# A squared relu moved from PSUM to SBUF, two copies moved to another engine, and the order of interleaved jobs changed, in an RWKV-7 and feed-forward kernel

## The chip, the cores and the metric

The kernel runs on one core of one Trainium2 chip. The metric is the device time of one execution in microseconds (us). A result is the median of several executions, with the lowest and highest beside it. Times are compared only between kernels that ran in turn on the same chip in the same rounds. All executions reported here were of the fast state.

Five engines work side by side: PE (TensorE, with PEld for its weight loads), DVE (VectorE), ACT (ScalarE), POOL (GpSimd) and SP, which here only issues transfers.

## The reference

There are two stages. A recurrence runs over 768 steps for 4 batches and 8 heads with head size 40. Then a feed-forward layer works on the 3072 tokens that come out of it.

```python
for t in range(S):
    y[:, :, t] = einsum('bhd,bhde->bhe', rt, state)
    Sa = einsum('bhde,bhe->bhd', state, at)
    state = state * wt[:, :, None, :] - einsum('bhd,bhe->bhde', Sa, bt)
    state = state + einsum('bhd,bhe->bhde', vt, kt)
x = y.transpose(0, 2, 1, 3).reshape(3072, 320)
h = maximum(x @ w_in, 0)          # w_in: 320 x 2048
out = (h * h) @ w_out             # w_out: 2048 x 320
```

## The kernel before

The sequence is cut into chunks of 128 steps, so there are 24 pairs of chunk and batch. The main loop takes them one after the other in 24 *slots*. A slot runs several generators, called jobs here, in twelve steps. In each step the jobs take their turns in the order of the list, so the list sets the order of instructions in every engine's queue.

```python
    for i in range(len(order)):
        n, begin = share.get(i, (10, 0))
        g = ready.pop(i)
        jobs = [(chain(i, g), 11, 0, TOTAL) if i else (first_slot, 10, 0, TOTAL)]
        if i + 1 < len(order):
            if i:
                ready[i + 1] = {}
                load(i + 1, ready[i + 1])
            jobs.append((rest(i + 1, ready[i + 1]), 9, 2, TOTAL))
        made = ahead.get(i, ())
        for j, m_ in enumerate(made):
            jobs.append((prepare(m_), 5, j * 5, TOTAL - 5 * (len(made) - 1 - j)))
        done.update(made)
        jobs.append((some(second, n), n, begin, TOTAL))
        # ... (one more piece in the first slots)
        weave(*jobs)
```

- `chain(i)` is the serial part of this chunk: products with a precomputed inverse T, two pairs of copies to `minus_x`/`xr`, the masked product RX, the outputs y. For y it needs RX and this chunk's own RV, which `rest` made one slot earlier.
- `rest(i + 1)` makes what the next chunk needs: kvT, the masked products A and RV, the state's update.
- `prepare(m)` makes the decay factors of a later chunk. What it makes goes to POOL, which solves for the inverses T of several chunks at a time and writes them out (`kept_t`).
- `some(second, n)` is a piece of the feed-forward layer. Slots 0 to 3 have none.

The feed-forward piece and the copies, before:

```python
                ps = [psum(ps_f ...)[:, :GB * C] for _ in range(2)]        # two PSUM banks
                for e, p_ in enumerate(ps):
                    mm(p_, w_third[half, ...], t_[half, NT, :], True)       # half-height: two at a time
                for e, p_ in enumerate(ps):
                    for j in range(NT):
                        mm(p_, w_in[:, j, ...], t_[:, j, :], False)
                    h_ = hidden[:, f + e]
                    nc.scalar.activation(h_, p_, Act.Relu)                  # L663
                    nc.vector.tensor_tensor(h_, p_, h_, Alu.mult)           # L664: reads the bank again
# in chain:
            nc.scalar.copy(xn[halves[half], ::2, :D], xs[halves[half]])             # L592
            nc.vector.tensor_copy(xn[halves[half], 1::2, :D], xs[halves[1 - half]]) # L593
# in rest:
        nc.vector.tensor_tensor(kT, kT_, down[:, :, 1:C + 1], Alu.mult)     # L503: kvT
```

In the profile's lines `L87` is the helper `mm`, `L311` the transposing helper, and `L327` the helper that masks A, RV and RX.

## Time and profile before

| | before |
|---|---|
| median of 3 runs (range) | 1071.65 us (1070.01 to 1072.65) |
| profiled span, mean granted clock | 1071.7 us, 0.904 |
| PE held up at w_third by the product L664 | some 30 groups, 21.5 us |
| PE held up by RX's masks | 22 waits of weight loads, 22.3 us |
| stretches at half clock between 310 and 960 us | 8 |

The page cuts the span into 40 slices of 26.8 us and gives the busy tenths of each. PEclk is the granted TensorE clock in tenths of full speed. Three rows of the kernel before:

```profile
PE   6267656769999999999999999999999999999898
POOL 4788555885886899932999921999958860000000
PEclk8657655688999999899899999999999999999899
```

PE is full from the tenth slice on, so from there PE's order and stalls set the time. POOL works in bursts up to the thirty-third slice; it is no bound as long as its inverses come in time. The isolated 8 in PEclk are slices in which the clock was halved for a while. PE does not become idle there, but slower. The prediction below shows the other lines.

### The profile page before, as it was taken

To read this page: it belongs to the slowest core of one execution; us is meant where nothing else is said; L and a number is where in the kernel's file an instruction comes from. 1 tells how busy PE (TensorE), PEld (TensorE's weight loads), DVE (VectorE), ACT (ScalarE), POOL (GpSimd) and SP (SyncE) were. 2 spreads that over 40 slices of the span, in tenths; PEclk is the share of its full clock that TensorE was granted. 3 is DMA by queue.
4 is the path that set the end of the run, shared out by engine and by line. 5 is a ranking of instruction groups with operands and counts; after the bars stand their busy time and mean duration, and the time that the engine had idled before them with its cause. 6 is when DMAs were issued, how large, how long until landed. Compare 5 with 4: busy or idle time off the path is not lost.

```text
span 1071.7 us, 19693 instructions
## 1 busy us (share of the span) xinstructions
PE 952.1 (89%) x7824; PEld 678.6 (63%) x7824; DVE 498.6 (47%) x1012; ACT 251.9 (24%) x555; POOL 650.2 (61%) x1124
## 2 busy tenths in 40 slices
PE   6267656769999999999999999999999999999898
PEld 5256546656677666776677666766676677667556
DVE  5448775796564265243452553452432432331120
ACT  3124241442321223113212222112212221231120
POOL 4788555885886899932999921999958860000000
PEclk8657655688999999899899999999999999999899
DMA  8978988759749616339437338335244332330000
GB/s 109 161 139 177 182 216 145 168 139 173 131 106 184 125 38 108 103 75 189 112 41 152 99 64 175 87 83 113 56 107 105 70 75 52 72 59 7 22 1 19
DMA packets 261356, 113.51 MB, mean 106 GB/s; under 512 B 243792, under 2 KB 249424, under 8 KB 259600
## 3 DMA queue, kind: packets, MB, share of 16 engines
q1 hardware_dynamic: 256928, 93.24, 44.6%
q0 software_dynamic: 3248, 18.88, 7.3%
q8 instruction: 62, 1.02, 0.4%
q10 hardware_dynamic: 1088, 0.13, 0.1%
q14 instruction: 30, 0.25, 0.1%
HBM read 75.77 MB, written 34.48 MB: 103 GB/s over the span
## 4 chain that ended last, share of the span: by engine, by line
PE 74%; DVE 11%; DMA 6%; issue 3%; POOL 3%; ACT 2%; SPq 2%; DVEq 0%; ACTq 0%; POOLq 0%
PE ps_f L87 38%; PE ps_c L87 14%; PE ps_w L87 14%; PE ps_w L311 4%; DVE decay L352 2%; DMA blocks<-kept_t 2%; DVE decay L353 2%; DMA dec<-kept_e 1%; DVE RX L327 1%; POOL half_t L434 1%; POOL half_p L432 1%; DMA in_k<-in_k_dram 1%; PE ps_w L531 1%; PE ps_c L577 1%; DMA w_out<-in_moe_w_in_dram 1%
## 5 line engine op out<-in xcount | busy, mean ns | idle before, releaser
L432 POOL TENSOR_TENSOR half_p<-half_n,half_t 128x70 f32<-128x70 f32 (+52 forms) x502 | 288.8, 575 | 100.2 <-DMA half_n<-kept_d 51.1
L434 POOL TENSOR_TENSOR half_t<-half_t,half_p 128x70 f32<-128x70 f32 (+52 forms) x502 | 314.0, 626 | 39.3
L87 PE MATMUL ps_f<-w_out,hid 128*128 128x320 f32 x672 | 204.8, 450 | 0.0
L87 PE MATMUL ps_f<-tokens,w_in 128*128 128x384 f32 x448 | 173.7, 512 | 0.0
L664 DVE TENSOR_TENSOR hid<-ps_f,hid 128x384 f32<-128x384 f32 x112 | 62.1, 555 | 202.5 <-ACT hid L663 202.4
L87 PEld LDWEIGHTS ps_f<-w_out,hid 128*128 128x128 f32 x672 | 124.8, 195 | 47.4 <-issue 6.0
L87 PEld LDWEIGHTS ps_f<-tokens,w_in 128*128 128x128 f32 x448 | 78.2, 194 | 65.4 <-issue 35.0
L663 ACT ACTIVATE hid<-ps_f 128x384 f32<-128x384 f32 x112 | 54.9, 491 | 261.7 <-PE ps_f L87 261.7
L593 DVE COPY minus_x<-ps_c 64x160 f32<-64x160 f32 x48 | 15.5, 322 | 143.8 <-ACT minus_x L592 143.0
L87 PE MATMUL ps_f<-tokens,w_third 64*128 64x384 f32 x224 | 75.6, 552 | 0.8 <-DVE hid L664 0.8
L87 PE MATMUL ps_w<-rT,kvT 40*128 40x128 f32 x384 | 38.9, 322 | 18.8 <-DVE RX L327 17.0
L87 PE MATMUL ps_w<-decay,bT 40*128 40x128 f32 x352 | 29.4, 312 | 21.5 <-DVE decay L357 18.4
L87 PEld LDWEIGHTS ps_w<-rT,kvT 40*128 40x128 f32 x384 | 32.3, 219 | 24.1 <-DVE RX L327 22.3
L409 POOL DMA_DIRECT2D half_n<-kept_d x18 | 8.9, 503 | 63.2 <-DMA kept_d<-N 62.9
L87 PEld LDWEIGHTS ps_c<-xr,T 64*64 64x64 f32 x768 | 29.1, 146 | 26.6 <-issue 20.5
L636 DVE TENSOR_TENSOR tokens<-ps_c,dec 128x512 f32<-128x512 f32 x24 | 16.5, 689 | 58.1 <-PE ps_c L87 58.1
L87 PEld LDWEIGHTS ps_w<-decay,bT 40*128 40x128 f32 x352 | 24.9, 212 | 28.5 <-issue 19.0
L327 DVE TENSOR_TENSOR A<-ps_w,upper 128x512 f32<-128x512 f32 x48 | 30.9, 684 | 22.4 <-PE ps_w L87 22.4
L87 PEld LDWEIGHTS ps_f<-tokens,w_third 64*128 64x128 f32 x224 | 28.0, 195 | 18.1 <-DVE hid L664 13.0
L87 PE MATMUL ps_c<-xr,T 64*64 64x40 f32 x768 | 35.0, 240 | 4.3 <-ACT xr L581 2.1
L352 DVE RECIPROCAL decay<-decay 128x256 f32<-128x256 f32 x22 | 38.3, 1739 | 0.0
L353 DVE RECIPROCAL decay<-decay 128x256 f32<-128x256 f32 x22 | 37.2, 1691 | 0.0
(140 smaller groups left out, 1433.5 us busy)
## 6 DMA issues: line engine op xcount, KB each, us to landing
kept_e<-decay SPq DMA_DIRECT2D x22, 780.0 KB
dec<-kept_e SPq DMA_DIRECT2D x22, 780.0 KB
hid<-in_moe_w_out_dram SPq DMA_DIRECT2D x16, 320.0 KB
half_n<-kept_d POOLq DMA_DIRECT2D x12, 384.0 KB, 9.5
half_n<-kept_d POOLq DMA_DIRECT2D x6, 768.0 KB, 9.6
in_w<-in_w_dram SPq DMA_DIRECT2D x24, 160.0 KB
in_ab<-in_b_dram SPq DMA_DIRECT2D x24, 160.0 KB
in_ab<-in_a_dram SPq DMA_DIRECT2D x24, 160.0 KB
```

The source lines that it names most:

```text
L87: nc.tensor.matmul(o, l_, r_, start=start, stop=True, skip_group_check=True)
L311: nc.tensor.transpose(p_[:, q * 128:(q + 1) * 128], pair(x_, q), ident)
L327: nc.vector.tensor_tensor(t_, p_, over4(upper), Alu.mult)
L352: nc.vector.reciprocal(down[:, :, MID + 1:C + 1], up[:, :, MID + 1:C + 1])
L353: nc.vector.reciprocal(up[:, :, :MID], down[:, :, :MID])
L432: nc.gpsimd.tensor_tensor(p_, part[:, at:at + m_].unsqueeze(1).to_broadcast([128, n, m_]), t3[:, :n, s:s + 1].to_broadcast([128, n, m_]), ...
L434: nc.gpsimd.tensor_tensor(t3[:, :n, s + 1:], t3[:, :n, s + 1:], p_, Alu.subtract)
L531: nc.tensor.transpose(p_[:, q * 128:(q + 1) * 128], down[:, q, 1:C + 1], ident)
L593: nc.vector.tensor_copy(xn[halves[half], 1::2, :D], xs[halves[1 - half]])
L636: nc.vector.tensor_tensor(t_, y_, g["up"][:, :, :C], Alu.mult)
L663: nc.scalar.activation(h_, p_, Act.Relu)
L664: nc.vector.tensor_tensor(h_, p_, h_, Alu.mult)
```

## The change

There are three parts. The squaring reads the relu's result in SBUF instead of the bank in PSUM, so that the bank is free once the relu is done. ACT makes both copies of each pair. And the list of jobs becomes chain, feed-forward, prepare, rest: the next chunk's part, second in each step so far, comes last.

```diff
-            nc.vector.tensor_copy(xn[halves[half], 1::2, :D], xs[halves[1 - half]])
+            nc.scalar.copy(xn[halves[half], 1::2, :D], xs[halves[1 - half]])
 ...
-        nc.vector.tensor_copy(xr[first, 1::2], x_[first, 1::2])
+        nc.scalar.copy(xr[first, 1::2], x_[first, 1::2])
 ...
-                    nc.vector.tensor_tensor(h_, p_, h_, Alu.mult)
+                    nc.vector.tensor_tensor(h_, h_, h_, Alu.mult)
 ...
         jobs = [(chain(i, g), 11, 0, TOTAL) if i else (first_slot, 10, 0, TOTAL)]
+        jobs.append((some(second, n), n, begin, TOTAL))
+        made = ahead.get(i, ())
+        for j, m_ in enumerate(made):
+            jobs.append((prepare(m_), 5, j * 5, TOTAL - 5 * (len(made) - 1 - j)))
+        done.update(made)
         if i + 1 < len(order):
             ...
             jobs.append((rest(i + 1, ready[i + 1]), 9, 2, TOTAL))
-        made = ahead.get(i, ())
-        for j, m_ in enumerate(made):
-            jobs.append((prepare(m_), 5, j * 5, TOTAL - 5 * (len(made) - 1 - j)))
-        done.update(made)
-        jobs.append((some(second, n), n, begin, TOTAL))
```

## The prediction

> **What bounds the kernel now.** I read the page first, then the table of busy time by stretch, then the sums of waits, then the timeline inside one slot. (A slot is the outer step for one chunk of one batch; twelve steps weave the chunk's own chain, the "rest" of the next chunk, the "prepare" of a later one and a piece of the feed-forward.) The page and two stretches (columns: stretch; busy us and instructions of PE, PEld, DVE, ACT, POOL; granted clock; DMA share; GB/s):
>
> ```profile
> PE 952.1 (89%) x7824; PEld 678.6 (63%) x7824; DVE 498.6 (47%) x1012; ACT 251.9 (24%) x555; POOL 650.2 (61%) x1124
> ```
>
> ```profile
> 100.00:200.00 100.00, 63.36 (x690) 54.25 (x690) 70.48 (x141) 34.85 (x77) 61.45 (x150) 0.64 0.84 177
> ...
> 600.00:700.00 100.00, 97.77 (x783) 67.49 (x783) 41.56 (x86) 23.17 (x51) 52.66 (x80) 0.97 0.55 122
> ```
>
> Before about 250 us the kernel waits for DMA and DVE and the clock is mostly half. From 250 to 1005 TensorE sets the time: it looks 97 to 100% busy. But a matmul's modelled duration (432 ns for 320 columns) is longer than the distance at which the next one starts (269 ns), so stalls hide under "busy". In the timeline one w_third group takes 846 ns up to the first w_in, undisturbed, because its half-height matmuls run two at a time; held up, it takes about 1490:
>
> ```profile
> 613.11 0.92 PE L87 MATMUL ps_f<-tokens,w_third 64*128 64x384 f32 x4
> ```
>
> ```profile
> 617.72 0.49 ACT L663 ACTIVATE hid<-ps_f 128x384 f32<-128x384 f32 x1 [1.30 <-PE ps_f L87]
> 618.20 1.56 PE L87 MATMUL ps_f<-tokens,w_third 64*128 64x384 f32 x4
> 618.24 0.56 DVE L664 TENSOR_TENSOR hid<-ps_f,hid 128x384 f32<-128x384 f32 x1 [1.61 <-ACT hid L663]
> 618.85 0.29 PEld L87 LDWEIGHTS ps_f<-tokens,w_third 64*128 64x128 f32 x2 [0.36 <-DVE hid L664]
> ```
>
> The second pair starts at 618.85, when the DVE product has left the bank; the relu was done at 618.21. The sums of waits, two more places in the timeline:
>
> ```profile
> PEld ps_w L87 <- DVE RX L327: 22.3, 22, 3.2
> PE ps_w L87 <- DVE RX L327: 17.0, 12, 3.0
> PEld ps_f L87 <- DVE hid L664: 13.0, 29, 1.1
> ```
>
> ```profile
> 674.18 1.16 PE L87 MATMUL ps_w<-rT,xnT 40*128 40x128 f32 x16
> 675.37 1.29 DVE L327 TENSOR_TENSOR RX<-ps_w,upper 128x512 f32<-128x512 f32 x2 [1.00 <-PE ps_w L87]
> 676.12 1.75 PE L87 MATMUL ps_w<-rT,kvT 40*128 40x128 f32 x16 [0.78 <-DVE RX L327]
> ```
>
> ```profile
> 677.80:682.00 4.20, 4.20 (x12) 2.80 (x12) 1.72 (x3) 0.00 (x0) 3.81 (x6) 0.59 0.00 0
> ```
>
> The RV products of the next chunk follow the chain's RX products directly and need RX's banks, so they wait for its masks on DVE; right after, the clock is halved for most of 4 us (the eight w_out matmuls there are up to 533 ns apart, not 269).
>
> **What the Trainium skill says.** (1) "SBUF — State Buffer", Who interferes with whom: a DVE instruction with two SBUF inputs contends with a GpSimd instruction that reads SBUF, and the later one fully blocks. The trace agrees. The only such product now is L524:
>
> ```profile
> L524 DVE TENSOR_TENSOR state<-state,f x40: 316/324/1211, 219.7 to 969.4; 64x160 f32<-64x160 f32 x40
> ```
>
> Undisturbed it takes 317 to 325 ns; arriving inside a POOL instruction it ends some 180 ns after that one's end, up to 1211. (2) "VectorE: DVE Perf Modes", The perf-mode tier table: fp32 tensor_tensor stays at 1x in SBUF, so squaring there gains no speed; the trace has 318 ns with a PSUM input (L617) and 320 without at the same 64x160. (3) "TensorE: Matmul & The Clock Gate", What's actually happening: the clock is halved or full by activity in free-running windows of 3.4 us. The trace's low stretches are multiples of 3.41 us; eight of them, between 347 and 726 us, come with RX/RV stalls.
>
> **The change part by part.**
>
> *Square in SBUF.* The bank is freed by the relu, not by the product. The last w_in of a pair issues at 0, the relu runs 0.52 to 1.01 us, the product to 1.61. Next w_third comes at 1.07 or later where the chain's small matmuls lie between, at 0.85 in the tightest order. So the wait goes in the first case and shrinks to about 0.2 us in the second. By the timeline the groups over 846 ns are: 18 x 0.644 + 8 x 0.80 + three early ones, 3.4, + 0.1 = 21.5 us. **Gain 20.** Cost: the product (112 by the page at 555 ns) now has two SBUF inputs. While POOL runs (250 to 877 us) it waits for the rest of a POOL instruction (half of about 1 us) plus about 0.41 (180 + 224 more elements at 1/0.96 ns): estimate 0.9 us. DVE at 42% can carry 0.35 x 90 = 32 us more, but it is later in line. POOL loses 0.25 us per product (estimate: 0.015 or 0.15 at L524, with 0.23 us more of reading): 9 us over the 32 products before 467. POOL is continuous up to there; chunk 10's inverse, written at 472.5 and loaded in 5, is needed at 495.7, so 18 us of slack allow a gain of 9 to 11 there.
>
> *ACT makes both copies.* 72 copies leave DVE (48 at 322, 24 at 310 ns: 22.9 us) for ACT (286 ns: 20.6). Both engines have room. DVE's copy anyway followed ACT's, so a pair saves 0.07 us, except where DVE was late:
>
> ```profile
> 242.78 1.07 PE L87 MATMUL ps_c<-minus_x,N 64*64 64x40 f32 x14 [3.57 <-DVE minus_x L593]
> ```
>
> That is 3.6 us; with smaller ones before 250, where a DMA often ends last, **gain 5**.
>
> *Rest last.* In the built order of PE, the feed-forward piece now comes between RX and RV (2.3 us, which covers RX's masks of 1.3). Removed: in slots 6 to 15 the stalls (0.9 to 1.9 at RV's start, 0.7 to 1.4 inside it) and the slow clock after, added over the slots, **35 us**. But rest's pieces now stand right ahead of the chain's, and on DVE behind the feed-forward product. Three new waits, in slots where a w_in piece is in front:
> - A after minus-x's transposes: the kvT product (0.69) now queues behind the square. From the last w_in: relu 1.01, square to 1.6 or 2.0, kvT to 2.3 or 2.7; PE is there at 0.86. Stall 1.6; the built order has it ten times: 16.
> - RV, then y directly. DVE must do the square, f and state (0.36 + 0.65 to 1.5) and RV's masks (1.29) while PE has only RV and sd (1.16 + 1.0). Stall 1.2 to 1.9, with 0.6 to 1.0 at RV where the reciprocals (3.43) come later too: seven slots x 2.3 + three x 1.4 = 20. Eight slots with w_out in front: 0.3 each, 2.4.
> - Some 15 stalls of over 1.2 us; if six in ten halve the clock at 1.6 us each: 15.
> Sum 53 against 35: **loss 19.**
>
> Total: 20 + 5 - 19 = 6 us, so 1066. All the errors I can see in the new waits make them too large (I let them add up, though a wait lets DVE catch up with the next), so I put the centre at **1060**.
>
> **The rivals.** (a) The reordering works: masks hide under the feed-forward piece, few new waits, the clock stays full. For: the stalls removed are certain. Then 20 + 5 + 25 less POOL's limit of 10: about 1032 to 1045. (b) New waits take over, and POOL's lock makes the square 1.2 us and more: DVE becomes the pace-maker of w_in slots, 1070 to 1080. (c) POOL becomes the bound near slot 10: late inverses, PE idle there, and only the gain after it counts: 1055. (d) Bank waits were hidden anyway: against it, a held-up group takes 0.64 us more, with nothing beside it.
>
> **Range and chances.** Eight in ten: 1042 to 1077, from (a)'s slower half to (b). Two per cent is 1050 or less: that needs the new waits at half of my estimate, 0.28. Slower by 2% is 1093: 0.05.
>
> **What the new profile would show.** PEld waiting for DVE hid near 0 and w_third groups at 846 ns: bank step right. L664 with a mean near 0.8 us and a minimum near 0.55: lock step right. Waits of PE for DVE RX small, new ones for DVE kvT and DVE RV, some 16 and 20 us: reorder step right; if these are under 10 us together, the prediction is too slow. A wait for the load of T in slot 10: (c). The stretch before 250 us moving by over 10 us either way would make it wrong as well.

## The result and the profile after

The changed kernel took **1059.95 us** (1059.48 to 1061.82, 4 runs) against 1072.15 (1070.01 to 1073.67, 4 runs) of the kernel before in the same rounds. The ratio is 0.9891, with a 95% interval of 0.987 to 0.9912: 1.1% faster, inside the 2% that counts as the same. A ratio here is worked out from the fast runs of both kernels in the same rounds, so it is not quite the ratio of the medians quoted. Where gains are compared across calls below, "us by ratio" means (1 - ratio) x 1070. That gives 11.7 for the change.

The page of the changed kernel, with the same rows as before and its table of busy time, has:

```profile
PE 943.7 (89%) x7824; PEld 684.2 (65%) x7824; DVE 500.5 (47%) x940; ACT 272.4 (26%) x627; POOL 668.4 (63%) x1124
...
PE   6375767778999999999999999999998999999898
...
POOL 4788564885898699981899952999958980000000
PEclk8656555578889999999999999999999999999899
```

The isolated 8s of PEclk in the middle of the run are gone, but six of the first twelve slices have lower clocks than before. POOL works 18.2 us longer for the same 1124 instructions.

The sums of waits of the changed kernel (engine, line, releaser: us in total, times, longest):

```profile
PEld ps_w L87 <- DVE kvT L503: 20.7, 13, 3.2
...
PEld ps_w L87 <- DVE RX L327: 8.8, 10, 2.5
```

```profile
PE ps_w L87 <- DVE kvT L503: 17.1, 11, 2.8
```

The wait of PEld ps_f for DVE hid is absent. PEld's wait for RX fell from 22.3 to 8.8. The wait for kvT is new in its size: before, it was 6.6 us in 4 waits for PEld and 5.3 in 2 for PE, all before 209 us. The groups, by busy time and mean, first one of the kernel before and then two of the changed kernel, and the durations of the changed L664 alone (min, median, max):

```profile
L87 PE MATMUL ps_f<-tokens,w_third 64*128 64x384 f32 x224 | 75.6, 552 | 0.8 <-DVE hid L664 0.8
```

```profile
L664 DVE TENSOR_TENSOR hid<-hid 128x384 f32<-128x384 f32 x128 | 92.5, 723 | 242.1 <-ACT hid L663 242.0
L87 PE MATMUL ps_f<-tokens,w_third 64*128 64x384 f32 x224 | 56.0, 539 | 3.2 <-DVE w_out L261 3.2
```

```profile
L664 DVE TENSOR_TENSOR hid<-hid x128: 494/559/1532, 247.1 to 1029.6; 128x384 f32<-128x384 f32 x128
```

The w_third groups take 56.0 us busy instead of 75.6, and PE no longer waits for hid there. The product has a median of 559 ns (558 before), but its slowest takes 1532. Before, the slowest of all 128 took 559: 112 read a bank of ps_f, the last 16 one of ps_w.

The timeline where the new wait arises (start, duration, then the instruction; in brackets the idle time before it and what ended it):

```profile
380.65 1.56 PE L87 MATMUL ps_f<-tokens,w_in 128*128 128x384 f32 x4
...
382.25 0.49 ACT L663 ACTIVATE hid<-ps_f 128x384 f32<-128x384 f32 x1 [1.74 <-PE ps_f L87]
...
382.77 0.66 DVE L664 TENSOR_TENSOR hid<-hid 128x384 f32<-128x384 f32 x1 [1.14 <-ACT hid L663]
...
383.35 0.68 DVE L503 TENSOR_TENSOR kvT<-ps_w,dec 128x512 f32<-128x512 f32 x1
...
384.08 1.16 PE L87 MATMUL ps_w<-dec,kvT 40*128 40x128 f32 x16 [1.44 <-DVE kvT L503]
```

DVE takes its queue in order. It sat idle for 1.14 us waiting for the relu, did the square, and only then the kvT product, whose own inputs had been there. PE stood for 1.44 us.

To see where time went, I cut each trace at the starts of slots, that is at the moments at which ACT makes the chain's first copy (L572). Durations in us of the profiled executions:

| | to slot 4 | slots 4, 5 | slots 6 to 15 | slots 16 to 22 | slot 23 and the end | span |
|---|---|---|---|---|---|---|
| before | 233.5 | 89.0 | 416.2 | 242.4 | 90.6 | 1071.7 |
| after | 233.7 | 95.4 | 390.6 | 248.1 | 90.4 | 1058.2 |

So 25.6 us were gained in slots 6 to 15, and 6.4 were lost in slots 4 and 5 and 5.7 in slots 16 to 22. The total of 13.5 for these two executions is the sum of large opposite terms, and the experiments are there to separate them.

### The profile page after: what moved, and what is told of

Read it like the earlier page. It is cut to its first block, busy times and chain, and to the rows that moved or that the text cites. A ratio compares the mean times of both kernels' runs of the same rounds, so it can differ in the third digit from the quotient of the medians.

```text
span 1058.2 us, 19794 instructions
## 1 busy us (share of the span) xinstructions
PE 943.7 (89%) x7824; PEld 684.2 (65%) x7824; DVE 500.5 (47%) x940; ACT 272.4 (26%) x627; POOL 668.4 (63%) x1124
## 4 chain that ended last, share of the span: by engine, by line
PE 74%; DMA 8%; DVE 7%; issue 3%; ACT 3%; POOL 3%; SPq 2%; DVEq 0%; ACTq 0%; POOLq 0%
PE ps_f L87 36%; PE ps_c L87 16%; PE ps_w L87 15%; PE ps_w L311 4%; SPq L108 2%; DMA dec<-kept_e 2%; DMA w_out<-in_moe_w_in_dram 1%; POOL half_t L434 1%; POOL half_p L432 1%; PE ps_c L577 1%; DMA in_b<-in_b_dram 1%; DVE decay L352 1%; DMA tokens<-tokens 1%; DMA in_w<-in_w_dram 1%; DVE decay L353 1%
## 5 line engine op out<-in xcount | busy, mean ns | idle before, releaser
L434 POOL TENSOR_TENSOR half_t<-half_t,half_p 128x70 f32<-128x70 f32 (+52 forms) x502 | 323.3, 644 | 39.3
L664 DVE TENSOR_TENSOR hid<-hid 128x384 f32<-128x384 f32 x128 | 92.5, 723 | 242.1 <-ACT hid L663 242.0
L87 PE MATMUL ps_f<-tokens,w_third 64*128 64x384 f32 x224 | 56.0, 539 | 3.2 <-DVE w_out L261 3.2
L348 DVE TENSOR_TENSOR_SCAN decay<-ps_w,ones 128x64 f32<-128x64 f32 x88 | 23.5, 267 | 51.0 <-PE ps_w L311 51.0
L87 PE MATMUL ps_w<-dec,kvT 40*128 40x128 f32 x384 | 31.9, 309 | 17.1 <-DVE kvT L503 17.1
L327 DVE TENSOR_TENSOR RX<-ps_w,upper 128x512 f32<-128x512 f32 x48 | 30.8, 682 | 33.5 <-PE ps_w L87 33.3
L503 DVE TENSOR_TENSOR kvT<-ps_w,dec 128x512 f32<-128x512 f32 x24 | 16.4, 684 | 58.4 <-PE ps_w L311 37.5
L87 PEld LDWEIGHTS ps_w<-dec,kvT 40*128 40x128 f32 x384 | 27.0, 210 | 22.2 <-DVE kvT L503 19.8
L327 DVE TENSOR_TENSOR RV<-ps_w,upper 128x512 f32<-128x512 f32 x48 | 30.9, 685 | 15.8 <-PE ps_w L87 15.4
L87 PE MATMUL ps_w<-rT,xnT 40*128 40x128 f32 x384 | 35.1, 293 | 3.6 <-ACT rT L513 2.9
```

The costliest lines, as they stand in the source:

```text
L87: nc.tensor.matmul(o, l_, r_, start=start, stop=True, skip_group_check=True)
L327: nc.vector.tensor_tensor(t_, p_, over4(upper), Alu.mult)
L348: nc.vector.tensor_tensor_scan(up[:, q, MID + 1:C + 1], wT[:, q, MID:], ones, 1.0, Alu.mult, Alu.mult)
L434: nc.gpsimd.tensor_tensor(t3[:, :n, s + 1:], t3[:, :n, s + 1:], p_, Alu.subtract)
L664: nc.vector.tensor_tensor(h_, h_, h_, Alu.mult)
```

## The experiments

My theory after the two traces was that the square and ACT's copies gain what was predicted, and that the new order removes the RX stalls but pays nearly as much in a new stall, because kvT stands behind the square in DVE's queue. The rivals were that POOL's lock or POOL itself sets the end, that the reorder costs in any case, and that the early slots move by chance.

Every kernel gave correct results. The table has the results and the stretches of each profiled execution, in the columns of the table above.

| kernel | median us (range, runs) | ratio (95%) | to 4 | 4, 5 | 6 to 15 | 16 to 22 | 23, end |
|---|---|---|---|---|---|---|---|
| sq_only | 1052.21 (1046.54 to 1054.36, 4) | 0.9834 (0.9786 to 0.9882) | 234.7 | 85.5 | 402.7 | 237.1 | 91.2 |
| act_only | 1065.43 (1058.26 to 1069.03, 20) | 0.9953 (0.9933 to 0.9973) | 231.9 | 85.1 | 416.4 | 242.3 | 90.6 |
| order_only | 1066.63 (1063.02 to 1072.17, 20) | 0.9971 (0.9954 to 0.9987) | 229.0 | 96.5 | 397.5 | 250.1 | 89.5 |
| sq_act | 1050.39 (1048.12 to 1051.75, 4) | 0.9828 (0.9796 to 0.986) | 235.5 | 84.3 | 404.5 | 236.2 | 89.6 |
| sq_order | 1061.88 (1058.4 to 1066.87, 11) | 0.9939 (0.9917 to 0.9962) | 230.1 | 97.2 | 394.2 | 251.2 | 90.7 |
| kvt_first | 1049.47 (1045.54 to 1050.86, 4) | 0.982 (0.9783 to 0.9858) | 230.2 | 95.0 | 388.8 | 244.2 | 90.3 |
| step8 | 1045.38 (1042.64 to 1048.17, 4) | 0.9789 (0.9745 to 0.9834) | 232.3 | 84.9 | 392.9 | 242.7 | 90.5 |
| after_actsq | 1037.77 (1035.11 to 1039.78, 4) | 0.9722 (0.9685 to 0.976) | 231.3 | 87.9 | 387.5 | 239.9 | 89.5 |
| step8_actsq | 1032.98 (1030.16 to 1035.41, 4) | 0.9678 (0.9646 to 0.9711) | 231.0 | 84.4 | 384.8 | 238.0 | 90.2 |
| late_order | 1057.07 (1049.64 to 1057.56, 4) | 0.9889 (0.9846 to 0.9931) | 235.8 | 81.4 | 398.6 | 249.1 | 90.6 |
| old_actsq | 1042.03 (1036.84 to 1050.67, 4) | 0.9751 (0.9683 to 0.9819) | 235.8 | 82.7 | 404.1 | 235.7 | 90.7 |
| late_actsq | 1036.22 (1036.05 to 1037.85, 4) | 0.9693 (0.9654 to 0.9733) | 231.6 | 82.0 | 390.2 | 239.6 | 91.1 |

### The parts alone: sq_only, act_only, order_only

Each is the kernel before with one part of the diff above: the line L664, the two lines of copies, or the list of jobs.

> The kernel before with the square taken in SBUF and nothing else. Theory (the bank wait was 21.5 us of hidden stalls, PE sets the pace): w_third groups at 846 ns, PE's load waiting for DVE hid near 0, the RX to RV stalls and the half-clock stretches after them unchanged; 1072 - 18 to 20, so 1052 to 1054 us. Rival (the bank wait was hidden, or POOL's lock on the square gives it back as later masks): 1066 to 1074. In both L664 rises from 556 ns to about 0.7 to 0.8 us on average.

> The kernel before with the 72 copies moved from DVE to ACT alone. Theory (only the late copy at 242 us and some small ones were on the path): 1 to 5 us faster, 1067 to 1071. Rival (DVE's queue held the chain up in many slots): 10 us faster or more. Second rival (ACT queues the second copy behind nothing, so no effect): 1071 to 1073.

> The kernel before with the order of the jobs changed alone. Theory after reading the changed kernel's trace (RX to RV stalls and half-clock stretches, 35 us by the prediction, go; new waits for the kvT product, about 1.4 us in ten slots, come; the first six slots lose a few us): bank waits stay or change place, 1055 to 1065. Rival (the prediction's sum, the reordering loses 19): 1085 to 1095. The granted clock after 310 us tells: full throughout by the theory, a dozen dips by the rival.

The square alone gained 17.8 us by ratio, and ACT's copies alone 5.0. The new order alone gained 3.1. In act_only the gain lies ahead of slot 6 (5.5 us in the first two columns), as predicted.

The waits of PE's loads for the product in order_only, which still squares from PSUM:

```profile
PEld ps_f L87 <- DVE hid L664: 5.9, 13, 0.5
```

Before, it was 13.0 us in 29 waits. So the new order halves the bank waits by itself, and the square and the order overlap: their gains must not be added.

### Pairs: sq_act and sq_order

sq_act is the change without the new list. sq_order is the change without ACT's copies.

> Square in SBUF and both copies on ACT, old order of the jobs. Theory (parts add): sq_only's and act_only's gains together, 1048 to 1052, with the RX to RV stalls and eight or so half-clock stretches between 340 and 730 us still there. If the prediction was right that the reordering loses, this is faster than the whole change (1060) by some 10 us or more; if the reordering gains, it is slower than 1060.

> The changed kernel with the copies given back to DVE. Theory (copies are worth 2 to 5 us as in the old order): 1061 to 1065. Rival (under the new order DVE's queue makes the copies late, behind the square): 1068 to 1075.

sq_act is **faster than the whole change**: 18.4 us by ratio against 11.7, with intervals that do not overlap. So the new order costs some 7 us when the other two parts are there (10 by the medians). The stretches show its two signs, from sq_act to the changed kernel: 11.1 us lost in slots 4 and 5, 13.9 gained in 6 to 15, 11.9 lost in 16 to 22. sq_order is 5.1 us slower than the change, the worth of ACT's copies once more. Beside the square in the old order they brought less: sq_act gained 0.6 us more than sq_only, which the intervals (some 3 and 5 us to either side) leave open.

In sq_act, and in sq_only as well, POOL's lateness already cost PE time in slot 10. The inverse for chunk 10 was written only at 482.0 us in sq_act (472.5 before); SP, which takes its queue in order, issued the load of T then and that of in_r at 488.3, and PE stood for it:

```profile
PE ps_w L311 <- DMA in_r<-in_r_dram: 4.1, 1, 4.1
```

Of the 13.9 us that the new order gained in slots 6 to 15, 6.1 lie in this slot (43.7 us in sq_act, 37.6 in the changed kernel), so they are not all RX stalls.

### kvt_first: the same order on PE, another on DVE

In step 5 of slots 4 and later, `rest` is called ahead of the feed-forward piece. This leaves the order on PE as in the changed kernel and puts only kvT, with the small copy that follows it, ahead of the square on DVE (in the two traces the 7824 instructions of PE have the same order, and on DVE only these change places).

```diff
-            for gen, n, at, to in gens:
+            for gen, n, at, to in other if other and step in (5,) else gens:
 ...
+            at = 2 + len(made)
+            other = [jobs[0], jobs[at], *jobs[1:at], *jobs[at + 1:]]
```

> The changed kernel, with the rest's part ahead of the feed-forward piece in step 5 of slots 4 to 22, so that on DVE the kvT product comes before the square; TensorE's order is the same. Theory (the wait for kvT, 1.41 us or more in ten slots, 17 us in all, is DVE's queue behind the square): those stalls go, 1060 - 12 to 15, so 1045 to 1048, or less where POOL's inverses then end last. Rival (the stall only moves, to RX's or RV's masks behind the late square, or DVE is busy anyway): 1055 to 1062, with new waits for DVE RX or RV.

PE's waits for kvT (17.1 us in 11 waits in the changed kernel):

```profile
PE ps_w L87 <- DVE kvT L503: 1.8, 1, 1.8
```

The kernel is 7.6 us faster than the change by ratio. The queue order on DVE alone therefore made the kvT stall. In this kernel PE began to wait for POOL's results instead (3.4 us for T until 792 us, 3.1 until 501 for a load behind T), and part of the 17 us was lost there.

### step8: only the step of RX and RV reordered

This is sq_act, but in step 8 of slots 4 to 22 the order is chain, feed-forward, prepare, rest. So the feed-forward and prepare come between RX and RV in this step, and the other steps keep the old order.

```diff
-            for gen, n, at, to in gens:
+            for gen, n, at, to in other if other and step in (8,) else gens:
 ...
+            other = [jobs[0], jobs[-1], *jobs[2:-1], jobs[1]]
```

> Square in SBUF, copies on ACT, old order of the jobs, but in step 8 of slots 4 to 22 the feed-forward piece and prepare come ahead of the rest's RV. Theory (of the reordering only this step pays; it takes away 16 us of RX to RV stalls and 8 to 10 us of half clock, and brings no kvT wait): 1050 - 15 to 22, so 1028 to 1035 without POOL's limit, 1035 to 1042 with it (waits for in_r or T at slots 10 and 18). Rival (the stalls move to y, which then follows RV directly, as the prediction sized at 20 us): 1045 to 1052.

It took 1045.38 us, the fastest so far. The slots up to 9 became shorter, and then a wait appeared:

```profile
PE ps_c L87 <- DMA T<-kept_t: 13.7, 2, 10.1
...
PE ps_w L87 <- DVE RX L327: 5.4, 2, 2.8
```

The RX wait is down from the 15.9 us of sq_act to two early ones. From 473.1 us PE stood 10.1 us for T, since POOL's inverse for chunks 10 to 13 was written only at 479.6. In the kernel before it was written at 472.5, but slot 10 started later too. Here POOL is the bound, as rival (c) of the prediction had it. In the changed kernel slot 10 starts at 487.0, so its inverse, written at 479.3, was in time.

### after_actsq and step8_actsq: the square on ACT

These are the changed kernel and step8 with one line changed. The square then neither stands in DVE's queue nor meets POOL.

```diff
-                    nc.vector.tensor_tensor(h_, h_, h_, Alu.mult)
+                    nc.scalar.activation(h_, h_, Act.Square)
```

> The changed kernel with the square done by ACT instead of DVE: it no longer stands ahead of the kvT product in DVE's queue and no longer holds or is held by a POOL instruction. Theory: the ten kvT stalls (17.5 us in the changed kernel) shrink to under 5, POOL's busy time falls from 668 back to about 650 and chunk 10's inverse lands near 472 instead of 479; 1045 to 1050 us. Rival: ACT, with 63 us more work on top of 272, gets late with its relu and its copies, and TensorE waits for ACT instead of DVE; 1055 to 1065 us.

> The fastest kernel so far (square, ACT's copies, the new order only in the step of RX and RV) with the square on ACT. Theory: that kernel is held by POOL (TensorE waits 10.2 us for T at 471.6), and the square's share of it is the shared port: without it chunk 10's inverse lands near 472 to 475 instead of 479.6, the wait falls to under 6 us, and the time to 1036 to 1041 us. Rival: the port is not what makes POOL late; the wait stays near 10 us and the time at 1043 to 1047.

after_actsq took 1037.77 us, 18 us less than the change by ratio and better than either theory had it. PE's order of instructions is the same. The run takes away the place in DVE's queue and the lock together, and does not say what each was worth. Page and durations:

```profile
PE 940.6 (91%) x7824; PEld 683.0 (66%) x7824; DVE 409.3 (40%) x812; ACT 336.3 (32%) x755; POOL 649.2 (63%) x1124
```

```profile
L664 ACT ACTIVATE hid<-hid x128: 522/523/529, 244.8 to 1007.5; 128x384 f32<-128x384 f32 x128
```

```profile
PE ps_w L87 <- DVE kvT L503: 1.2, 1, 1.2
```

The square takes 522 to 529 ns on ACT whatever else runs. POOL is back at 649.2 us (668.4 with the square on DVE). The kvT stalls are gone. The chunk-10 inverse was written at 474.0 instead of 479.3. Of the gain, 7.5 us lie in slots 4 and 5 and 8.2 in slots 16 to 22. In slots 6 to 15 only 3.1 were left, because slot 10 took 42.8 us instead of 37.6: PE was now early enough to wait for POOL's inverse and for a load, with half clock after it (495.3 to 502.1).

In step8_actsq the wait for T went from 13.7 us in 2 waits to this:

```profile
PE ps_c L87 <- DMA T<-kept_t: 2.2, 1, 2.2
```

The inverse was written at 469.6 instead of 479.6, with 1032.98 us in total. Of these 10 us, 7.8 are a shorter busy time of the same 723 POOL instructions up to that write (365.4 us in step8, 357.6 here). So DVE's square, through the lock, and not POOL's own work, was most of what made POOL late in step8. This is the fastest kernel of the study: 3.2% less than the kernel before.

### old_actsq: what the reorder is worth without a square in DVE's queue

This is sq_act with the square on ACT: the old list of jobs.

> The square and both copies on ACT with the old order of jobs. It prices the reorder where no square stands ahead of the kvT product. Theory: DVE's queue is what made the new order cost 10 us (1050.4 against 1060.0 with the square on DVE); with the square on ACT its sign turns, so this kernel is slower than the new order with the square on ACT (1037.8) by the RX stalls and their half clock: 1045 to 1050 us, with PE waiting for RX some ten times. Rival: the new order costs something in any case, and ACT's square alone is the gain; 1030 to 1037.

The four runs were 1036.84, 1037.15, 1046.90 and 1050.67 us, so the result is **inconclusive as to the sign**: the ratio of 0.9751 has an interval that covers that of after_actsq (0.9722). Neither theory's range was met by the median. A loss of 7 us or more, as the order made with the square on DVE, lies just outside what the two intervals allow. The profiled run is the longest of the four (granted clock 0.902 and 0.908 in the longer two, 0.912 and 0.916 in the others), so what follows from it holds for a long run. It has the RX stalls and six stretches at half clock between 310 and 960 us:

```profile
PE ps_w L87 <- DVE RX L327: 15.1, 12, 2.7
```

From this trace to after_actsq the order gains 16.6 us in slots 6 to 15 and loses 5.2 in slots 4 and 5 and 4.2 in slots 16 to 22. No kvT stalls are left there. A wait for T is 1.2 of the 4.2, and I did not find what the rest is.

### late_order and late_actsq: the old order in the first six slots

In slots 0 to 5 the list is the old one, with the square on DVE and on ACT respectively.

```diff
-        jobs.append((some(second, n), n, begin, TOTAL))
+        if i >= 6:
+            jobs.append((some(second, n), n, begin, TOTAL))
 ...
+            parts.insert(len(parts) if i >= 6 else 0, (rest(i + 1, ready[i + 1]), 9, 2, TOTAL))
+        jobs += parts
+        if i < 6:
+            jobs.append((some(second, n), n, begin, TOTAL))
```

> The changed kernel, but its first six slots keep the old order of jobs. Theory: the new order is what made those slots longer (slot 6 starts at 329.1 us instead of 322.5); with the old order there and the square in SBUF it starts near 321 to 324 and the kernel takes 1051 to 1056 us. Rival: the early slots move by chance or by the square; 1058 to 1062 us. A third way: slot 6 starts early, and POOL's inverse for chunk 10 takes the gain back as a wait for T near slot 10.

> The new order from slot 6 on, the old one before, with the square on ACT. Theory: slot 6 starts at 315 to 318 us (319.2 with the new order everywhere) since the order's early cost was mostly the DVE square in slots 4 and 5; the wait for POOL's inverse near slot 10 takes that back, so 1034 to 1038 us. Rival: the early order costs 12 us by itself, as late_order against the changed kernel says (317.2 against 329.1), and slot 6 starts at 310 or earlier.

late_order's slot 6 started at 317.2 us instead of 329.1, earlier than expected. So the new order did cost the early slots their time. Slot 5 in both traces (stretch; busy us and instructions of PE, PEld, DVE, ACT, POOL; granted clock; DMA share; GB/s), first the changed kernel, then late_order:

```profile
284.20:329.10 44.90, 42.96 (x349) 30.35 (x350) 26.32 (x49) 12.21 (x29) 40.27 (x60) 0.91 0.52 102
```

```profile
277.90:317.20 39.30, 38.14 (x349) 26.98 (x349) 25.32 (x49) 12.10 (x28) 35.30 (x52) 1.00 0.65 137
```

It is the same work on PE, in 39.3 us instead of 44.9, without the half clock. Yet **the total did not follow**: the ratio is 0.9889 against 0.9891 of the change. From slot 6 to slot 15 late_order took 398.6 us against 390.6. Its kvT stalls were as long as those of the change or longer (1.34 to 2.29 us), but the clock was halved after five of them (at 413, 611, 693, 840 and 912 us), and in the change after one of ten (948 us).

Why one stall halves the clock and the next of the same length does not can be read from the traces' clock records. Between 150 and 1000 us of every trace, all changes of the granted clock lie within 0.01 us of a grid of 3.413 us, and the grid lies differently from execution to execution (its first point comes 0.03 to 3.35 us after the start of the span). The four kernels with kvT stalls (the change, order_only, sq_order, late_order) have 29 of 1.33 or 1.34 us after slot 6 began. The 7 that began between 0.13 us before a point of the grid and 0.71 after it were followed by half clock, and the other 22, which all began elsewhere, were not. Of the 11 longer ones, 6 were, in a somewhat wider stretch of the grid. So for a stall of this length the place on the grid decided, which is chance from one execution to the next. How busy PE was around the stall may count too; that was not tested.

One of the four runs took 1049.64 us, which would be the whole gain, but it has no trace.

In late_actsq slot 6 started at 313.6 (theory 315 to 318, rival 310), against 319.2 in after_actsq. Half of these 5.6 us were given back in slot 10 (45.5 us instead of 42.8), which waited for POOL again. Its time of 1036.22 is as the theory had it.

With the square on DVE, slots 4 and 5 took 95 to 97 us in every kernel that has the new order there (after, order_only, sq_order, kvt_first), and 81 to 89 in those with the old order. With the square on ACT the new order took 87.9. From sq_act to the change the new order costs 11.1 us there, from old_actsq to after_actsq 5.2: about half of the early loss comes from the new order together with DVE's product, the rest from the order alone. The halves lie in different slots. Slot 4 took 50.5 us in the change and 45.0 in sq_act; in it PE waits 3.2 us at a w_third for the last rounding of the weights (L261), and so it does in after_actsq (3.3), but not in sq_act or old_actsq, which have the old order. (order_only, whose copies are DVE's, has a wait of 3.7 us for such a copy there instead.) Slot 5 took 44.9 and 39.3; with the square on ACT it took 38.8 in both orders.

## Why the prediction was right, and where its steps were not

The predicted time was 1060.0 and the measured one 1059.95, inside the range and in the class given the highest chance. That it agrees to 0.1 us is luck. The steps gave 1066, the 1060 was a judgement, and four terms were wrong in ways that partly cancel. Two slips in the sums change little: 53 - 35 is 18, and 32 products at 0.25 us are 8.

1. **The bank step was right.** Predicted gain 20, sq_only 17.8. The PEld wait for hid is gone, and in sq_only most groups take 0.84 to 0.90 us and nine 1.05, the "about 0.2" that was left in the tighter order.
2. **The lock step was right in kind, a little large in size.** Predicted mean of the product near 0.8 us, with the minimum at 0.55; measured 0.723, and 0.494. POOL was expected to lose 0.25 us per product. It lost 18.2 us in the 84 products that overlap its instructions (counted in the trace), about 0.2 each. These 84 took 809 ns on average, the other 44 took 558, and 56 of the 72 that began inside a POOL instruction ended 409 to 420 ns after its end, where the prediction had 0.41 us. The chunk-10 inverse came 6.8 us later, where 9 were expected. One reading was not right: L524 was not the only such product before, since L521, also with two inputs in SBUF, took up to 1189 ns against a median of 153.
3. **ACT's copies were right.** Predicted 5, measured 5.0 alone and 5.1 with the rest, but only 0.6, within a wide interval, on top of the square in the old order.
4. **The kvT wait was right.** Predicted ten stalls of 1.6, in sum 16. The trace has ten after slot 6 began, of 1.33 to 1.97 us by the view of waits; counted from start to start, less the 0.20 us of a slot without a stall, they are 1.41 to 2.05 and in sum about 15. With one of 2.8 at 167 us the view gives 17.1 for all. kvt_first shows the cause: put ahead of the square on DVE, the wait disappears.
5. **What the order removes was over-sized.** The prediction put the RX stalls and the slow clock after them at 35 us, and the new waits apart. The runs leave it between about 16 and 22. From sq_act to the change slots 6 to 15 gained 13.9, with five kvT stalls of together 7.9 us in them, so 21.8 were removed (small new waits taken off), or 15.7 without the 6.1 of slot 10, where sq_act waited for a load behind T. From old_actsq to after_actsq they gained 16.6, with 5.9 us lost in slot 10 to loads behind T and half clock (42.8 against 36.9), so 22.5; but this old_actsq trace is that of the longest of four runs.
6. **The step "RV, then y directly" had a wait that does not exist.** It was put at 20 + 2.4. In the code y reads the RV of its own chunk, made one slot earlier, and not the RV whose masks DVE makes in this step. The trace has it so: DVE begins the masks after PE has begun y's products with RV.

```profile
512.16 1.16 PE L87 MATMUL ps_c<-rT,sd 128*128 128x128 f32 x8
...
513.25 1.09 PE L87 MATMUL ps_c<-RV,in_k 128*64 128x128 f32 x16
...
513.88 1.29 DVE L327 TENSOR_TENSOR RV<-ps_w,upper 128x512 f32<-128x512 f32 x2
```

   In the view of waits no instruction of PE waits for RV at all. At the start of RV, where 0.6 to 1.0 was predicted, the first matmul comes 0.36 to 0.50 us after the one ahead of it, some 2 to 3 us in all slots together. So this is not a wait that DVE caught up with, as the prediction's own doubt had it, but a false dependency.
7. **The half-clock term was mis-sized in the changed kernel.** It was put at 15 us, six of ten stalls halving the clock. In the changed kernel one of ten did, in order_only three, in sq_order four, in late_order five: 13 of 40. So the term is real, but six in ten was too many, and, as the clock records under late_order show, which stall is hit depends on where it falls on the grid. That it was only one in the changed kernel was luck.
8. **The early slots were left out of the sum.** It had no term for what the new order does in slots 4 and 5. There it cost 11.1 us (sq_act to the change), and old_actsq and after_actsq show that DVE's product makes about half of it.
9. **POOL as the bound, rival (c), did not decide this kernel.** In the changed kernel the only wait for T is 1.5 us. It costs the faster ones time: sq_only, sq_act, kvt_first, step8, after_actsq, step8_actsq and late_actsq all wait in slot 10 for T or for a load behind it (3.3 to 12.8 us in sum).

The reorder's own account was predicted at -19. Measured from sq_act to the change, it is -7 by ratio and -10 by the medians. By the stretches of the two traces it is 21.8 removed (the 6.1 of slot 10 among them), less 7.9 and 7.0 of kvT in slots 6 to 15 and 16 to 22, less 11.1 in slots 4 and 5, less 4.9 more in slots 16 to 22, which makes -9.1. The half clock at 948 and the wait of 1.5 us for T are in these 4.9; the rest of them is not attributed.

## What to carry to other kernels

Before moving a job in an interleaved schedule, check in the code which slot each input comes from, and follow each engine's queue, not only the one that is the bound: the reorder was right for PE and wrong for DVE, where a waiting square blocked a product that PE needed, and one line that moved the square to the mostly idle ACT (26% busy) turned a gain of 1.1% into 2.8%. Judge parts of a change with the others present and absent, for here the new order gained 3 us alone and lost 7 to 10 beside the other two. And look for the next supplier in line (here POOL's inverses) before counting a gain, since everything gained ahead of it may be spent waiting for it.

## What the Trainium skill lacked or had wrong

- "SBUF — State Buffer", Who interferes with whom, states the exclusive lock between a DVE instruction with two SBUF inputs and a GpSimd instruction that reads SBUF, and the runs agree, but it gives no cost for such a stream. Here the 128 products went from at most 559 ns to a mean of 723 and a maximum of 1532, 56 of the 72 that began inside a POOL instruction ended 409 to 420 ns after it, and POOL's busy time rose from 650.2 to 668.4 us. Moved to ACT, the square took 522 to 529 ns and POOL was back at 649.2, as the section's sentence on PE and ACT has it.
- "TensorE: Matmul & The Clock Gate", What's actually happening, has the clock fall back after at least one idle window of about 3.4 us. Here half clock followed stalls of only 1.3 to 2.3 us, and not always: after 1, 3, 4 and 5 of ten such stalls in four kernels. For 29 stalls of 1.33 or 1.34 us, it depended on where they began on the 3.413 us grid of the clock's changes. The page's section on a second failure mode names micro-idles between groups, without a length.
- "ScalarE: Activation LUTs", Rules for kernel authors, sends multiplications to VectorE, for its lower cost per element in bf16. For this fp32 square of 128x384 ACT took 523 ns against 559 undisturbed and 723 on average on DVE, and the whole kernel became 18 us faster with it.
